# Token numbers written with each batch's placing, and a batch's first load of stage two in two parts

## The chip, the cores and the metric

One core of one Trainium2 chip runs the whole program in one launch. The metric is device time in microseconds (us). The kernel before took 594.89 us (median of three runs, 594.38 to 596.47).

## The reference

`x` (8 batches x 2496 x 256) is filtered along the sequence by FFT, and the 19968 rows that come out go through a mixture of eight experts, one expert for each row:

```python
X = np.fft.rfft(x, axis=1)
y = np.fft.irfft(X * (filt_r + 1j * filt_i)[None], n=2496, axis=1)
logits = y @ w_gate + modality_bias[modality_id]          # (19968, 8)
e = argmax(logits); gate_w = softmax(logits)[e]
out[row] = gate_w * (relu(y[row] @ w1[e]) @ w2[e])        # 256 -> 1024 -> 256
```

## The kernel before

The transform is split as 48 x 52 and runs batch by batch in three stages of matrix products. **Stage 1** (L208) multiplies pieces of `x` and stores the result to DRAM (`b1_d`), one store for every two pieces. A batch has 13 pieces, so its last store holds one piece alone: time steps 24 and 25. **Stage 2** (L532) loads `b1_d` back transposed in three chunks (`load_t2`, L456; partition = 4 x time step + quarter, so the last store's rows are partitions 96 to 103), goes forward (L476), multiplies by the filter and goes back (L488, L489). The result is stored to `b2_d` and loaded back by `load_t4` (L462). **Stage 3** (L551) finishes the transform into `yw`, one of two buffers `yws` (named yo_105 and yo_106 below, used by even and odd batches), and adds up the gate's logits.

Then a batch is **routed**. `counting` (L605) finds each row's expert on VectorE, `placing` (L630) gives every row its place in a bin of its expert, and 20 scatters (L678), issued by GpSimd, write the rows of `yw` into the bins `bins_d`. Beside 256 features a row of `yw` holds its token number, which line 635 writes as one GpSimd instruction over the buffer, and its gate. `tabling` makes a table of full blocks of 256 rows of one expert.

The **experts** take such blocks: SyncE loads one (`xs`, L756), TensorE turns it (L785), multiplies it up (L799, Relu on ScalarE) and down (L812), VectorE scales the result into `osb` (L819, three buffers), and GpSimd scatters it to the output (L821, two to a block) by the token numbers. A block's L819 cannot start until the scatters of the block three before it have landed.

In the main loop (from L1136) the batches overlap. Batch g begins its stage 1 at slot `begin[g]`, 14 slots after the one before; stage 2 follows 16 slots later (`OFF2`), its chunks are loaded two slots ahead (`LEAD`), and routing comes at slot 45. In each slot up to two or three scatters into the bins are traced and 1.5 steps of the experts, four steps to a block.

Up to the main loop the order on TensorE, VectorE and ScalarE is the written one. In the loop a list scheduler sets the order on every engine at build time. It moves an instruction forward as far as its dependencies allow. `paced` (L130) adds one: the instruction waits for the TensorE product traced last. Scatters into the bins and weight loads are paced; line 635 is not. Each engine, and each engine's queue of DMA issues, works in its own order, and an instruction that waits holds what stands behind it.

Of the kernel before, what the change touches and what calls it, by code (L numbers as in the profile page):

```python
# [13 lines left out]
BF16 = mybir.dt.float16  # L14
I32 = mybir.dt.int32
AF = mybir.ActivationFunctionType
ALU = mybir.AluOpType
# [12 lines left out]
def kernel(  # L30
# [12 lines left out]
    nc = tc.nc  # L43

    B, S, D = x.shape
# [12 lines left out]
    NS = N1 // 2  # L58
    NTT = N2 // 2
    KA = 2 * N1  # L60
    KB = 2 * N2
# [15 lines left out]
    DW = D // 2  # L77
# [36 lines left out]
    EV = 2  # L114
# [4 lines left out]
    SCH = 8  # L119
    xp = ctx.enter_context(tc.tile_pool(name="fx", bufs=3))  # L120
    rp = ctx.enter_context(tc.tile_pool(name="fr", bufs=2))
    bp = ctx.enter_context(tc.tile_pool(name="fbig", bufs=4))
# [7 lines left out]
    def paced(ins):  # L130
        tc.add_manual_dep(ins.ins, marks["pe"][-1].name,
                          mybir.DependencyInfo(mybir.DependencyClass.Sync, mybir.DependencyReason.DATA),
                          reason="pace")
# [18 lines left out]
    op = ctx.enter_context(tc.tile_pool(name="opsum", bufs=1, space=bass.MemoryType.PSUM))  # L152
# [35 lines left out]
    st = [dict() for _ in range(B)]  # L188
# [35 lines left out]
    def input_piece(g, k):  # L224

        stage1(g, k)
        if (k + 1) * EV in [t1 for t0, t1 in TCH]:
            load_x()
# [81 lines left out]
    with tc.manual_schedule():  # L310
# [102 lines left out]
        for s0 in range(0, NS, SPB):  # L413
            for src, dst in ((w2m, a1m), (w2x, a2m)):
# [8 lines left out]
                a = 0  # L423
                if s0 == 0:
                    nc.scalar.copy(dst[:, 0, :], tp[:KB, 0:KB])
                    a = 1
# [26 lines left out]
    tp_ = ctx.enter_context(tc.tile_pool(name="table", bufs=1))  # L453


    def load_t2(g, c):  # L456
        src = b1_d[g].rearrange("t (jr s) c -> (t jr) s c", jr=4)
        t2 = bp.tile([KB, SCH, D], BF16, tag="t24", name="t2")
        nc.sync.dma_start(t2, src[:, c * SCH:(c + 1) * SCH, :])
        st[g]["t2", c] = t2  # L460

    def load_t4(g, c):  # L462
        t0, t1 = TCH[c]
        src = b2_d[g].rearrange("s (jr t) c -> (s jr) t c", jr=4)
        t4 = bp.tile([KA, TCM, D], BF16, tag="t24", name="t4")
        nc.sync.dma_start(t4[:, 0:t1 - t0, :], src[:, t0:t1, :])
        st[g]["t4", c] = t4
# [64 lines left out]
    def stage2(g, k):  # L532

        if k < NK:
            ps = forward(g, k)
        if k > 0:
            pz = inverse(g, k - 1)
        if k < NK:
            filtering(g, k, taken(g, k, ps))
        if k > 0:  # L540
            returned(g, k - 1, pz)
# [88 lines left out]
    def placing(g):  # L630

        yw, lg = st[g]["yw"], st[g]["lg"]
        b3 = [P, NY, E]
        mx, ohT, sc, c = st[g]["route"]
        nc.gpsimd.tensor_single_scalar(yw[:, :, DW:DW + 1], tok, g * S, op=ALU.add)
        psO = pp.tile([P, 2, E], F32, tag="ps")
        nc.tensor.matmul(psO[:, 0, :], lhsT=Lexcl, rhs=c, start=True, stop=True)
        nc.tensor.matmul(psO[:, 1, :], lhsT=ones_sq, rhs=c, start=True, stop=True)
        nc.vector.tensor_sub(lg, lg, mx[:, :, None].to_broadcast(b3))
        nc.scalar.activation(lg, lg, AF.Exp)  # L640
        off = sp.tile([P, E], F32, tag="off")
        nc.vector.tensor_add(off, cnt, ecap)
        nc.vector.tensor_add(off, off, psO[:, 0, :])
        nc.vector.tensor_add(cnt, cnt, psO[:, 1, :])
        yield
        nc.vector.tensor_add(sc, sc, off[:, :, None].to_broadcast([P, E, NY]))
        nc.vector.tensor_mul(sc, sc, ohT)
        yield
        pos = sp.tile([P, NY], F32, tag="pos")
        nc.vector.reduce_sum(pos, sc.rearrange("p e t -> p t e"), axis=AX.X)  # L650
        pos_i = sp.tile([P, NY], I32, tag="posi", bufs=2)
        nc.vector.tensor_copy(pos_i, pos)
        st[g]["pos"] = pos_i
        yield
        ssum = sp.tile([P, NY], F32, tag="ssum")
        nc.vector.reduce_sum(ssum, lg, axis=AX.X)
        nc.vector.reciprocal(yw[:, :, DW + 1].bitcast(F32), ssum)
# [6 lines left out]
    def count(g):  # L664

        run(counting(g))

    def place(g):

        run(placing(g))  # L670
# [245 lines left out]
    def pace(left):  # L916

        if to_bins and left:
            g, t = to_bins[0]
            if t < NY:  # L920
                scatter(g, t)
                to_bins[0][1] += 1
                left -= 1
            else:
                if g == B - 1:
                    pad_bins()
                opening.append((g, n))
                to_bins.pop(0)
        return left


    def routed(g):

        place(g)
        to_bins.append([g, 0])

    def tabled(g):

        run(tabling(g, KR[g], g == B - 1))
# [8 lines left out]
    with tc.manual_schedule(engines={ET.PE, ET.Activation, ET.DVE}):  # L948
# [92 lines left out]
        tok = const_pool.tile([P, NY, 1], I32)  # L1041
# [36 lines left out]
        def routes(g):  # L1078

            yield from counting(g)  # L1080
            for _ in range(4):
                yield
            yield from placing(g)
            to_bins.append([g, 0])
            yield
            yield from tabling(g, KR[g], False)
# [20 lines left out]
        for k in range(LONG):  # L1107
# [4 lines left out]
            n += 1  # L1112
        some(-1)
        load_t2(3, 0)
        load_t4(2, 0)
        count(1)
# [11 lines left out]
    LEAD = 2  # L1128
# [7 lines left out]
    while n <= end or to_bins or opening:  # L1136
        if n == 0:
            routed(TURNED - 1)
        if n == 4:
            tabled(TURNED - 1)  # L1140
        for g in range(TURNED + 2, B):
            if 0 <= n - begin[g] < NP:
                input_piece(g, n - begin[g])
        for g in range(TURNED + 1, B):
            k = n - begin[g] - OFF2
            if (k + LEAD) % 4 == 0 and 0 <= k + LEAD < NS // EV:
                load_t2(g, (k + LEAD) // 4)
            if 0 <= k <= NS // EV:
                stage2(g, k)
        for g in range(TURNED, B):  # L1150
            k = n - begin[g] - OFF3
            if (k + LEAD) % 3 == 0 and 0 <= k + LEAD < NPY:
                load_t4(g, (k + LEAD) // 3)
            if 0 <= k <= NPY + 1:
                stage3(g, k)
            if k == NPY + 2:
                count(g)
            if k == NPY + 3:
                routed(g)
                tabled(g)  # L1160
        if n <= end:
            pace(pace(pace(3) if n < 8 else 2) if n % 2 or n < GAP else 1)
            owed += STEPS
        else:
            pace((n - end) % 3)
            owed += FT // FQ
        while owed >= 1:
            owed -= 1
            moe.step()
        n += 1  # L1170
# [43 lines left out]
```

## Time and profile before

| | |
|---|---|
| median of three runs | 594.89 us |
| profiled execution | 592.98 us |
| its span | 591.2 us |
| TensorE busy | 512.1 us (87%) |
| ScalarE, VectorE, GpSimd busy | 379.9, 377.6, 367.4 us |
| GpSimd's 160 scatters into the bins | 162.1 us busy |
| GpSimd's 158 scatters to the output | 160.1 us busy |

The profile's times are from the start of the span; 1.8 us of the execution lie outside of it. PE is TensorE, DVE VectorE, ACT ScalarE, POOL GpSimd and SP SyncE; a "q" behind a name is the engine's sequencer. In a row of the timeline the bracket gives how long the engine stood idle before the instruction and what ended it.

### The profile page before, as it was taken

What the parts mean: (1) busy time and instruction counts of PE and PEld (TensorE: products, weight loads), DVE (VectorE), ACT (ScalarE), POOL (GpSimd) and SP (SyncE); (2) the same over time, 40 slices, a digit from 0 to 9 for tenths busy, and PEclk for the clock granted to TensorE, in tenths of its full rate; (3) what the DMA queues carried; (4) which work ended last, traced back from release to release, by engine and by line L of the source; (5) the groups of instructions that cost most, each with busy time, mean ns of one, the idle gap of its engine ahead of it and who ended that gap; (6) DMA issues with size and microseconds to landing.
All of it is one profiled execution on the core that took longest, in us unless ns stands there. A gap on an engine that the chain in (4) does not pass through costs nothing.

```text
span 591.2 us, 16242 instructions
## 1 busy us (share of the span) xinstructions
PE 512.1 (87%) x5115; PEld 463.2 (78%) x5115; DVE 377.6 (64%) x1209; ACT 379.9 (64%) x693; POOL 367.4 (62%) x409
## 2 busy tenths in 40 slices
PE   3689986739969989999999989966999999999991
PEld 2677875628858888888888978855999999999991
DVE  8557986656766777769679777554555555555541
ACT  4578886827856877777876754433666666666660
POOL 8112336727746776774776776777777777655552
PEclk9969998969998998999998999978999999999997
DMA  8949999887697787898667463224444443333321
GB/s 152 184 68 192 197 212 208 180 204 209 160 239 208 203 198 222 231 211 241 184 176 204 139 165 112 87 86 146 137 127 123 119 125 122 118 109 110 99 73 33
DMA packets 69301, 93.29 MB, mean 158 GB/s; under 512 B 11427, under 2 KB 52841, under 8 KB 69059
## 3 DMA queue, kind: packets, MB, share of 16 engines
q0 software_dynamic: 21504, 50.75, 35.2%
q1 hardware_dynamic: 24409, 29.94, 20.1%
q10 hardware_dynamic: 23302, 11.50, 7.4%
q8 instruction: 48, 0.79, 0.6%
q14 instruction: 38, 0.31, 0.2%
HBM read 64.68 MB, written 46.35 MB: 188 GB/s over the span
## 4 chain that ended last, share of the span: by engine, by line
PE 46%; DMA 20%; issue 11%; POOL 9%; DVE 8%; ACT 3%; SPq 0%; POOLq 0%; DVEq 0%; ACTq 0%
PE hps L799 14%; PE ops L812 13%; POOL out_dram L821 5%; DMA t<-b_d 5%; DMA b_d<-t 3%; DMA bins_d<-yo,pos_i 3%; DMA b_d<-z 3%; PE ps L476 3%; DMA out_dram<-osb,meta 2%; DMA g<-g 2%; PE pz L488 2%; PE lt L584 2%; PE ps L569 2%; PE pz L489 2%; PE pT L785 2%
## 5 line engine op out<-in xcount | busy, mean ns | idle before, releaser
L804 ACT ACTIVATE hT<-hps 128x512 f16<-128x512 f32 x316 | 188.1, 597 | 120.7 <-PE hps L799 118.7
L799 PE MATMUL hps<-xT,w 128*128 128x256 f16 x1264 | 203.6, 282 | 5.7 <-DVE xT L786 5.6
L821 POOL DMA_INDIRECT out_dram<-osb,meta x158 | 160.1, 1014 | 76.4 <-DVE osb L819 36.6
L812 PE MATMUL ops<-w2sb,hT 128*128 x1264 | 198.5, 277 | 2.7 <-issue 2.5
L678 POOL DMA_INDIRECT bins_d<-yo,pos_i x160 | 162.1, 1013 | 56.6 <-issue 19.8
L799 PEld LDWEIGHTS <-w 128*128 128x128 f16 x1264 | 148.1, 146 | 11.0 <-DVE xT L786 6.0
L812 PEld LDWEIGHTS <-hT 128*128 128x128 f16 x1264 | 125.2, 99 | 18.9 <-issue 3.1
L819 DVE TENSOR_SCALAR osb<-ops,meta 128x256 f32<-128x256 f32 x158 | 69.4, 475 | 24.9 <-DMA out_dram<-osb,meta 17.3
L777 DVE COPY w<-w1sb 128x2048 f16 x79 | 56.2, 711 | 42.9 <-PE hps L799 41.1
L786 DVE COPY xT<-pT 128x512 f16<-128x512 f16 x79 | 33.4, 423 | 53.0 <-PE pT L785 52.3
L503 ACT CAST xf<-ps 104x512 f16<-104x512 f32 x96 | 56.9, 592 | 11.5 <-PE ps L476 9.5
L510 DVE TENSOR_TENSOR p<-xf,g 104x512 f16<-104x512 f16 x96 | 40.5, 421 | 36.7 <-ACT xf L503 35.8
L525 ACT CAST z<-pz 104x512 f16<-104x512 f32 x72 | 42.5, 590 | 9.7 <-PE pz L489 8.1
L476 PE MATMUL ps<-t,w2m 104*104 104x256 f16 x192 | 39.9, 292 | 8.7 <-DMA t<-b_d 7.9
L511 DVE TENSOR_TENSOR xf<-xf,g 104x512 f16<-104x512 f16 x96 | 40.5, 421 | 10.0 <-DMA g<-g 6.9
L488 PE MATMUL pz<-p,a1m 104*104 104x256 f16 x144 | 37.5, 284 | 2.7 <-DVE p L510 1.8
L218 ACT CAST t<-ps 96x512 f16<-96x512 f32 x52 | 30.1, 581 | 14.3 <-PE ps L214 12.8
L593 DVE COPY yT<-lt 128x512 f16<-128x512 f16 x80 | 33.5, 419 | 7.1 <-PE lt L589 6.3
L489 PE MATMUL pz<-xf,a2m 104*104 104x256 f16 x144 | 36.6, 280 | 0.0
L785 PE MATMUL pT<-ident,xs 128*128 128x128 f16 x316 | 32.8, 227 | 4.4 <-DMA xs<-bins_d 4.4
L144 POOL DMA_DIRECT2D xt<-in_x_dram x32 | 18.3, 573 | 28.7 <-PE fp L253 14.2
L584 PE MATMUL lt<-ident,yo 128*128 128x128 f16 x320 | 31.4, 221 | 3.7 <-ACT z L525 3.3
(206 smaller groups left out, 725.5 us busy)
## 6 DMA issues: line engine op xcount, KB each, us to landing
xs<-bins_d SPq DMA_DIRECT2D x79, 130.0 KB
xt<-in_x_dram POOLq DMA_DIRECT2D x24, 384.0 KB
t<-b_d SPq DMA_DIRECT2D x18, 384.0 KB
t<-b_d SPq DMA_DIRECT2D x15, 416.0 KB
b_d<-z ACTq DMA_DIRECT2D x30, 208.0 KB
b_d<-t ACTq DMA_DIRECT2D x24, 192.0 KB
w1sb<-in_moe_w_dram POOLq DMA_DIRECT2D x16, 256.0 KB
w2sb<-in_moe_w_dram POOLq DMA_DIRECT2D x8, 512.0 KB
```

Source lines behind the costliest of these rows:

```text
L476: mm = nc.tensor.matmul(ps[:KB, i, :], lhsT=w2m[:, s + i, :], rhs=st[g]["t2", s // SCH][:, s % SCH + i, :], start=True, stop=True)
L488: nc.tensor.matmul(pz[:KB, i, :], lhsT=a1m[:, s + i, :], rhs=p1[:, i, :], start=True, stop=False)
L489: nc.tensor.matmul(pz[:KB, i, :], lhsT=a2m[:, s + i, :], rhs=p2[:, i, :], start=False, stop=True)
L503: nc.scalar.copy(xf, ps[:KB])
L678: ins = nc.gpsimd.indirect_dma_start(out=bins_d[:, :], out_offset=IOA(ap=st[g]["pos"][:rows, t:t + 1], axis=0), in_=st[g]["yw"][:rows, t, ...
L777: cp = nc.vector.tensor_copy(b["w1"].rearrange("p a f -> p (a f)"), w1sb[:, ds(ej, 1)].rearrange("p o a f -> p (o a f)"))
L785: nc.tensor.transpose(pT[:, dc, i, :], xh[:, i, dc * P:(dc + 1) * P], ident)
L799: mm = nc.tensor.matmul(hps[:, k, :], lhsT=b["w1"][:, dc, ft:F:FT], rhs=b["xT"][:, dc].rearrange("p i t -> p (i t)"), start=(dc == 0), sto ...
L804: nc.scalar.activation(b["hT"][:, q * FQ:(q + 1) * FQ, :], hps, AF.Relu)
L812: nc.tensor.matmul(b["ops"][:, i, :], lhsT=b["hT"][:, ft, i * P:(i + 1) * P], rhs=w2sb[:, ds(b["ej"], 1), ft, :], start=(ft == 0 and i == ...
L819: nc.vector.tensor_scalar_mul(osb[:, i, :], b["ops"][:, i, :], gate[:, i, :])
L821: ins = nc.gpsimd.indirect_dma_start(out=out[:, :], out_offset=IOA(ap=b["meta"][:, i, 0:1], axis=0), in_=osb[:, i, :], in_offset=None, bou ...
```

## The change

Three edits. The token numbers' instruction gets `paced`. The load of stage two's first chunk, for the batches that are loaded in the main loop (4 to 7), becomes two: partitions 0 to 95 one slot sooner than the whole was, and partitions 96 to 103, which hold the last store's rows, in the slot of the old load. The other two chunks are loaded as before.

```diff
-    def load_t2(g, c):
+    def load_t2(g, c, part=None):
         src = b1_d[g].rearrange("t (jr s) c -> (t jr) s c", jr=4)
-        t2 = bp.tile([KB, SCH, D], BF16, tag="t24", name="t2")
-        nc.sync.dma_start(t2, src[:, c * SCH:(c + 1) * SCH, :])
-        st[g]["t2", c] = t2
+        if part != 1:
+            st[g]["t2", c] = bp.tile([KB, SCH, D], BF16, tag="t24", name="t2")
+        a, b = {None: (0, KB), 0: (0, KA), 1: (KA, KB)}[part]
+        nc.sync.dma_start(st[g]["t2", c][a:b], src[a:b, c * SCH:(c + 1) * SCH, :])
...
-        nc.gpsimd.tensor_single_scalar(yw[:, :, DW:DW + 1], tok, g * S, op=ALU.add)
+        paced(nc.gpsimd.tensor_single_scalar(yw[:, :, DW:DW + 1], tok, g * S, op=ALU.add))
...
             k = n - begin[g] - OFF2
-            if (k + LEAD) % 4 == 0 and 0 <= k + LEAD < NS // EV:
+            if k + LEAD in (-1, 0):
+                load_t2(g, 0, k + LEAD + 1)
+            if (k + LEAD) % 4 == 0 and 0 < k + LEAD < NS // EV:
                 load_t2(g, (k + LEAD) // 4)
```

TensorE, VectorE and ScalarE keep their orders, instruction for instruction. GpSimd and SyncE change.

GpSimd, where batch 3's scatters end (out of yo_106) and batch 4's begin (out of yo_105), before; `xt` is a load of `x`, TENSOR_SCALAR is the token numbers:

```order
L821 DMA out_dram<-osb,meta 19968x256 x2
L678 DMA bins_d<-yo_106,pos_i 162048x130
L635 TENSOR_SCALAR yo_106<-tok 128x20
L144 DMA xt<-in_x_dram 96x512
L821 DMA out_dram<-osb,meta 19968x256
L678 DMA bins_d<-yo_105,pos_i 162048x130 x2
```

and now:

```order
L824 DMA out_dram<-osb,meta 19968x256 x2
L681 DMA bins_d<-yo_106,pos_i 162048x130
L144 DMA xt<-in_x_dram 96x512
L638 TENSOR_SCALAR yo_105<-tok 128x20
L824 DMA out_dram<-osb,meta 19968x256
L681 DMA bins_d<-yo_105,pos_i 162048x130 x2
```

Before, batch 5's numbers went into the buffer that batch 3's last scatter had just been issued from; now batch 4's go into the other, whose scatters were issued a batch ago.

GpSimd, from batch 4's last scatters to batch 5's first, before:

```order
L678 DMA bins_d<-yo_105,pos_i 162048x130 x3
L821 DMA out_dram<-osb,meta 19968x256 x2
L678 DMA bins_d<-yo_105,pos_i 162048x130 x3
L635 TENSOR_SCALAR yo_105<-tok 128x20
L821 DMA out_dram<-osb,meta 19968x256 x2
L678 DMA bins_d<-yo_106,pos_i 162048x130 x5
```

and now:

```order
L681 DMA bins_d<-yo_105,pos_i 162048x130 x3
L824 DMA out_dram<-osb,meta 19968x256 x2
L681 DMA bins_d<-yo_105,pos_i 162048x130 x3
L638 TENSOR_SCALAR yo_106<-tok 128x20
L824 DMA out_dram<-osb,meta 19968x256 x2
L681 DMA bins_d<-yo_106,pos_i 162048x130 x5
```

The place is the same and the buffer is the other; so it is where batch 6 follows batch 5. Scatters and output scatters keep their order.

SyncE at batch 5's first load of stage two (`t`), before; `xs` are the experts' blocks, L754 and L757 read a block's number:

```order
L756 ISA
L756 DMA xs<-bins_d 128x260
L754 TENSOR_LOAD bj_i
L754 ISA x2
L459 DMA t_4234<-b_d 104x2048
L756 ISA
L756 DMA xs<-bins_d 128x260
```

and now:

```order
L759 ISA
L759 DMA xs<-bins_d 128x260
L463 DMA t_4145<-b_d 96x2048
L757 TENSOR_LOAD bj_i
L757 ISA x2
L463 DMA t_4145<-b_d 8x2048
L759 ISA
L759 DMA xs<-bins_d 128x260
```

The larger part goes ahead of the reading of a block's number, the small one stands where the whole load stood, and no load of `xs` is passed.

## Rows read from the trace of the kernel before

**Rows 1.** The page's chain that ended last: shares of the span by engine

```profile
PE 46%; DMA 20%; issue 11%; POOL 9%; DVE 8%; ACT 3%; SPq 0%; POOLq 0%; DVEq 0%; ACTq 0%
```

**Rows 2.** Waits, whole run: engine, line, waited for: us, times, longest

```profile
POOL yo L635 <- DMA bins_d<-yo,pos_i: 21.1, 5, 6.4
...
DVE osb L819 <- DMA out_dram<-osb,meta: 17.3, 8, 5.5
```

**Rows 3.** Timeline of TensorE: start, us, line, operation, [idle before <- releaser]

```profile
177.28 0.67 PE L476 MATMUL ps<-t,w2m 104*104 104x256 f16 x2 [3.67 <-DMA t<-b_d]
...
222.69 0.38 PE L476 MATMUL ps<-t,w2m 104*104 104x256 f16 x2 [2.68 <-DMA t<-b_d]
...
267.06 0.42 PE L476 MATMUL ps<-t,w2m 104*104 104x256 f16 x2 [0.72 <-DMA t<-b_d]
...
268.41 0.38 PE L476 MATMUL ps<-t,w2m 104*104 104x256 f16 x2
...
388.80 0.60 PE L637 MATMUL psO<-c,Lexcl 128*128 128x8 f32 x2 [5.33 <-DVE c L627]
...
404.39 0.60 PE L799 MATMUL hps<-xT,w 128*128 128x256 f16 x4
...
409.37 1.07 PE L799 MATMUL hps<-xT,w 128*128 128x256 f16 x4 [3.94 <-DVE xT L786]
```

**Rows 4.** Timeline of GpSimd, between one batch's scatters and the next's

```profile
268.61 1.05 POOL L678 DMA_INDIRECT bins_d<-yo,pos_i  x1 [0.30 <-PE ps L214]
276.06 0.32 POOL L635 TENSOR_SCALAR yo<-tok 128x20 int32<-128x20 int32 x1 [6.41 <-DMA bins_d<-yo,pos_i]
...
279.07 0.97 POOL L678 DMA_INDIRECT bins_d<-yo,pos_i  x1 [0.30 <-PE ps L476]
...
316.63 0.91 POOL L678 DMA_INDIRECT bins_d<-yo,pos_i  x1 [0.30 <-issue]
...
323.65 0.97 POOL L678 DMA_INDIRECT bins_d<-yo,pos_i  x1 [0.30 <-PE pT L785]
...
359.51 1.33 POOL L678 DMA_INDIRECT bins_d<-yo,pos_i  x1 [0.30 <-issue]
...
367.13 0.98 POOL L678 DMA_INDIRECT bins_d<-yo,pos_i  x1 [0.30 <-PE lt L589]
...
404.07 1.00 POOL L821 DMA_INDIRECT out_dram<-osb,meta  x1 [0.30 <-issue]
```

**Rows 5.** Timeline of VectorE: the experts' results and a batch's places

```profile
271.66 0.47 DVE L819 TENSOR_SCALAR osb<-ops,meta 128x256 f32<-128x256 f32 x1
...
315.53 0.17 DVE L652 CAST pos_i<-pos 128x20 int32<-128x20 f32 x1
...
355.79 0.17 DVE L652 CAST pos_i<-pos 128x20 int32<-128x20 f32 x1
...
384.67 0.88 DVE L819 TENSOR_SCALAR osb<-ops,meta 128x256 f32<-128x256 f32 x2 [4.41 <-DMA out_dram<-osb,meta]
...
407.95 0.88 DVE L819 TENSOR_SCALAR osb<-ops,meta 128x256 f32<-128x256 f32 x2 [5.51 <-DMA out_dram<-osb,meta]
```

**Rows 6.** Issue of batch 4's last store but one, on ScalarE's queue

```profile
161.74 0.31 ACTq L221 DMA_DIRECT2D b_d<-t  x1
```

**Rows 7.** The chain that ended last, in order of time: start, us, what

```profile
165.97 6.64 DMA b_d<-t
172.68 4.57 DMA t<-b_d
...
211.34 5.45 DMA b_d<-t
...
384.54 2.29 DMA bins_d<-yo,pos_i
```

**Rows 8.** Stretches: us, busy us (count) by PE, PEld, DVE, ACT, POOL; PEclk, DMA share, GB/s

```profile
160.00:182.00 22.00, 17.17 (x143) 14.41 (x141) 14.17 (x57) 12.95 (x25) 9.26 (x11) 0.87 0.97 252
...
410.00:500.00 90.00, 90.00 (x841) 83.62 (x839) 48.27 (x120) 55.52 (x93) 69.12 (x69) 0.97 0.42 127
```

## The prediction

> **What bounds the kernel now.** I read the chain that ended last first. TensorE holds 46% of it, DMA 20% and GpSimd 9% [rows 1]: products are the floor, and what can be won is where TensorE waits. From 410 to 500 us it is busy for 90.00 of 90 us [rows 8], and it stays so to its last products. So every us that TensorE loses before 410 is a us at the end, and only those count.
>
> TensorE's timeline shows the losses. At 177.28, 222.69 and 267.06 it waits 3.67, 2.68 and 0.72 us for the first load of stage two of batches 4, 5 and 6 [rows 3]. At 388.80 and 409.37 it waits 5.33 and 3.94 us for VectorE [rows 3]; a third such wait of about 1.2 us lies between them. VectorE's own timeline says why: at 384.67 and 407.95 it stood 4.41 and 5.51 us in front of L819 because an `osb` buffer was not yet scattered to the output [rows 5]. Over the run this wait comes to 17.3 us in 8 times [rows 2]. So GpSimd is late there, though its share of the chain is small.
>
> Its timeline tells where it fell behind. Between one batch's last scatter and the next one's first it stands still in front of the token numbers, 6.41 us at batch 4 and 21.1 us in 5 times [rows 2, 4], until the scatters just issued have let go of the buffer. Within a batch's scatters it never idles longer than the 0.30 us between two instructions, so from 279 us on it has no room to catch up.
>
> **The token numbers.** Eight instructions of about 0.3 us stay; what goes is the wait for a buffer's own scatters. The other buffer, which is now written, was scattered a batch ago. I give the first two of the five waits nothing: the scatters behind them start where their batch's places are made, and GpSimd has caught up when they end. I count the last three, from one scatter's end to the next batch's first scatter [rows 4]. With d for what TensorE is ahead by the stage-two loads:
>
> - Batch 4: 269.66 to 279.07. Now an `x` load (0.9), the numbers (0.6 with the gap) and one output scatter (1.29) stand between. That scatter needs the first half of the `osb` made at 271.66 to 272.13 [rows 5], so batch 4 starts at 273.8 - d. Gain 5.3 + d.
> - Batch 5: 317.54 to 323.65, 6.1 us. Numbers 0.6 and two output scatters 2.6 remain, so it would start at 315.4 - d, but the places are there at 315.70 - d [rows 5]. Gain then 7.9 + d.
> - Batch 6: 360.84 to 367.13, 6.3 us, against 3.2. The places come at 355.96 - d [rows 5], GpSimd at 356.1 - d. Gain then 11.0 + d.
>
> After it GpSimd runs the same scatters at the same pace, so the output scatter at 404.07 [rows 4] starts 11.0 + d sooner. The wait added is for a product. For batch 4 it is the product at 268.41 [rows 3], and GpSimd is there at about 269.7 - d or later; for batches 5 to 7 it comes later still against its product. Behind the waiting instruction stand an `x` load and output scatters, and VectorE waits for these; a late mark would cost its lateness. Bounds: 0, and 2 us where GpSimd is ahead; I take 0, since it is the one that is late.
>
> TensorE must be able to use it. Without late outputs it would get back 4.4 of the 5.33 us (I leave 0.9 for VectorE's counting, which it still has to await), 1.2 and 3.9. It runs at the lower of its two clock levels after each of the two long waits: four products take 1.07 us at 409.37 against 0.60 at 404.39 [rows 3], some 2 us lost each. That is about 14 us, more than 11.0, so GpSimd sets what is won. One wait remains in part: the `osb` wait at 407.95 would end at 407.95 - 11.0 - d, while VectorE gets there, at 402.44 before, about 4.4 + 1.2 + 2.5 + d sooner. That leaves some 2.6 us of the 5.51.
>
> **The load in two parts.** Now the last store takes 6.64 us to land, the load behind it 4.57 us, and TensorE starts [rows 7]. Of the load only 32 KB remain behind the store. No row shows so small a load. Bounds: 2.29 us, the landing of a 66 KB scatter [rows 7], and 4.57, the whole load. I take 2.4, near the scatter. The 384 KB ahead go off when the store before has landed: that one was issued at 161.74 [rows 6], so with 6.64 us they start at 168.4 and land by 173 to 175.
>
> What it costs: they now share the DMA with the last store, where the DMA share is 0.97 and 252 GB/s move [rows 8]. If the store lands behind all of them it is late by 384 KB / 252 GB/s = 1.6 us; if not, by nothing. I take 0.5. A rule bears on this. The Trainium skill ("DMA: Bandwidth & Descriptors", Queues, rings and completion order) says that each DMA engine goes round-robin between the queues that have work, a packet at a time, so loads and stores of two issuing engines take turns. By that rule the 96 KB store meets at most about its own size of the load, an estimated 0.4 us, and the sum below would be 16.3; with the store behind the whole load it would be 14.3. No row here shows the turns.
>
> Batch 4: 172.6 + 0.5 + 2.4 = 175.5 instead of 177.28, gain 1.8 (0.6 to 2.3). Batch 5: the store lands at 216.8 [rows 7], then 219.7; TensorE is free at 220.0, gain 2.6 (1.8 to 2.68). Batch 6: the wait of 0.72 goes. Batch 7 did not wait. d = 5.0, from 3.1 to 5.7. SyncE issues four loads more at about 0.4 us each and passes none by; reading a block's number now stands between the parts, and the wait for the store covers it.
>
> **Sum.** 11.0 + 5.0 = 16.0 us off 592.98, that is 577.0 for an execution like the profiled one. The median of the runs shown lies 1.9 us above it: 579.
>
> **Rivals.**
> A. The store is slowed by the load, or the small load takes as long as the whole: d = 0 and only GpSimd's part stays. For it: the DMA share of 0.97. Against it: 32 KB are half of the scatter that landed in 2.29 us. Gain 11.0, 584.
> B. GpSimd's lateness costs nothing that can be won, because the waits at 388.80 and 409.37 come back as others (counting, places, loads of blocks). For it: GpSimd is on only 9% of the chain. Against it: VectorE's waits name the output scatters. Only d stays: 590.
> C. Slower: scatters and output scatters that run 8 to 11 us sooner meet the stores and loads of stages one to three, whose pairs are on the chain (6.64 and 4.57 us at batch 4). If each of the four pairs that end a wait of TensorE grows by half, 5 us, that is 20 against 11, about 604. It decides from 2.8 us for each pair. Against it: the same bytes move, only sooner, and the share falls from 0.97 at 160 to 0.42 after 410 [rows 8].
> D. The change doesn't do what it says: GpSimd comes to the numbers before their product, and waits as long for it as it did for the scatters. Then 594 to 595. Against it: 268.41 lies ahead of GpSimd's arrival.
>
> **How the numbers follow.** Forecast 0.62, A 0.14, B 0.12, C 0.07, D 0.05. The forecast's own range is 573 to 584: TensorE's limit (14 + 5 + up to 2 of low clock after 177.28) below, d = 3.1 and some lateness above. To hold eight in ten it takes in A and part of B: 573 to 590. A measurement of this kernel can tell about 0.3%, 1.8 us, from no change. Faster by more: 0.88 (forecast, A, B); the same: 0.05 (D); slower: 0.07 (C).
>
> **What would show it.** GpSimd: no idle time over 1 us in front of the token numbers after 200 us, and 0.3 us for each of them. VectorE: waits for output scatters down from 17.3 to under 6 us. TensorE: the wait at batch 5's first stage-two products gone, batch 4's near 2 us, the one ahead of batch 7's counting near 1. Loads of 32 KB landing within 2.3 to 3 us of the last store. It would be wrong if TensorE still stood 3 us or more twice between 370 and 400, if the numbers waited for TensorE, or if the last store's landing grew by over 1.5 us.

## The result

The changed kernel takes 586.34 us (median of four runs, 584.62 to 587.38) where the kernel before takes 595.47 (four runs, 594.38 to 596.47): 0.984 of its time, 95% interval 0.981 to 0.988. It is faster, inside the stated range, and by 9.1 us where 16.0 were forecast. The profiled execution took 585.33 us with a span of 583.2, that is 7.7 and 8.0 us less than before.

On the chips of the experiments the kernel before varied more (585.89 to 601.13), so two medians that lie 2 us apart aren't told apart there by one series; the ratios leave the longest executions out as disturbed, in the first series 11 of the kernel before's 23, and so can lie nearer 1 than the medians do.

GpSimd first. In the changed kernel's waits (engine, line, waited for: us, times, longest) the 21.1 us in front of the token numbers [rows 2] are gone; two waits for TensorE's products, in the opening and at batch 2, remain. VectorE's waits for the output scatters stand almost as they were:

```profile
DVE osb L822 <- DMA out_dram<-osb,meta: 16.5, 10, 5.5
...
POOL yo L638 <- PE ps L214: 4.8, 1, 4.8
...
POOL yo L638 <- PE fp L214: 1.5, 1, 1.5
```

GpSimd's timeline in the changed kernel shows the starts of batches 4, 5 and 6 (L681 after L638), which answer to 279.07, 323.65 and 367.13 [rows 4]:

```profile
270.41 0.28 POOL L638 TENSOR_SCALAR yo<-tok 128x20 int32<-128x20 int32 x1
273.26 1.07 POOL L824 DMA_INDIRECT out_dram<-osb,meta  x1 [2.56 <-DVE ni L708]
274.63 1.07 POOL L681 DMA_INDIRECT bins_d<-yo,pos_i  x1 [0.30 <-issue]
...
313.00 0.28 POOL L638 TENSOR_SCALAR yo<-tok 128x20 int32<-128x20 int32 x1
...
317.00 0.97 POOL L681 DMA_INDIRECT bins_d<-yo,pos_i  x1 [1.09 <-issue]
...
354.90 0.28 POOL L638 TENSOR_SCALAR yo<-tok 128x20 int32<-128x20 int32 x1
...
357.97 1.08 POOL L681 DMA_INDIRECT bins_d<-yo,pos_i  x1 [0.30 <-PE ps L575]
```

The numbers take 0.28 us and wait for nothing. The three batches start 4.4, 6.7 and 9.2 us sooner.

TensorE's timeline in the changed kernel, at the places of [rows 3] and at a new one:

```profile
176.74 0.39 PE L479 MATMUL ps<-t,w2m 104*104 104x256 f16 x2 [2.29 <-DMA t<-b_d]
...
220.28 0.38 PE L479 MATMUL ps<-t,w2m 104*104 104x256 f16 x2 [1.83 <-DMA t<-b_d]
...
229.60 0.39 PE L572 MATMUL ps<-t,wbm 96*128 96x256 f16 x1 [3.41 <-DMA t<-b_d]
...
382.56 0.39 PE L640 MATMUL psO<-c,Lexcl 128*128 128x8 f32 x2 [0.85 <-DVE c L630]
...
399.88 1.07 PE L802 MATMUL hps<-xT,w 128*128 128x256 f16 x4 [3.74 <-DVE xT L789]
```

The 5.33 us at 388.80 have shrunk to 0.85 and the 0.72 us at batch 6 are gone. The waits at batches 4 and 5 are smaller. At 229.60 TensorE stands 3.41 us for the first load of stage three (`load_t4`), where the kernel before did not wait for the same product:

```profile
229.96 0.28 PE L569 MATMUL ps<-t,wbm 96*128 96x256 f16 x1
```

TensorE's order is the same in all the kernels here, so every product can be compared with itself. The table gives how much later (+) or sooner (-) than in the kernel before the same product starts, in us, for the products that started there at the times of the first row (388.8 is the one behind the wait of 5.33 us). It is worked out from the profiled executions, so each row holds an accident as well: at 150 us, before the waits in question, the rows lie between -1.9 and +1.4.

| | 150.3 | 228.1 | 245.0 | 268.1 | 350.8 | 388.8 | 415.1 | last |
|---|---|---|---|---|---|---|---|---|
| changed kernel | -1.1 | -3.9 | +0.4 | +0.2 | -0.4 | -6.2 | -10.6 | -9.7 |
| the same, again | -1.4 | -5.8 | +0.2 | -0.1 | -0.1 | -6.0 | -9.2 | -8.5 |
| token numbers only | -0.2 | +0.5 | +0.8 | +0.8 | +0.8 | -4.8 | -9.2 | -8.0 |
| load in two parts only | +0.4 | -2.5 | +2.2 | +0.7 | +1.0 | +0.6 | -2.0 | -0.9 |
| two parts, stage three's load ahead | +1.4 | +1.7 | +1.3 | +1.3 | +1.7 | -0.5 | -1.8 | -0.8 |
| changed, stage three's load ahead | -0.5 | -3.0 | -1.9 | -2.6 | -3.8 | -8.2 | -13.3 | -10.5 |
| the same, again | +1.4 | -1.6 | +0.5 | 0.0 | +1.2 | -4.5 | -11.2 | -6.8 |
| that, load in three parts | -0.4 | -4.9 | -2.8 | -3.3 | -2.5 | -7.6 | -12.3 | -12.0 |
| that in two parts, four osb buffers | +1.2 | -1.6 | -1.2 | -2.0 | -3.1 | -7.9 | -18.8 | -16.1 |
| before, four osb buffers | -1.5 | -1.2 | +3.0 | +2.5 | +2.3 | -1.4 | -8.0 | -3.6 |
| all edits | -1.9 | -3.8 | -3.5 | -3.9 | -4.6 | -9.1 | -20.3 | -16.6 |

The first two rows tell the story. What the load in two parts won by 228 us was gone at 245. All that remains was won between 350 and 415, and that is GpSimd's part.

Why the load at 229.60 was late can be read in the changed kernel. Its chain that ended last (start, us, what), which answers to 211.34 [rows 7], with SyncE waiting at the end of it:

```profile
209.86 6.49 DMA b_d<-t
216.37 0.02 SPq L463
216.41 3.82 DMA t<-b_d
...
222.64 0.18 SPq L759
...
223.72 5.83 DMA t<-b_d
```

and SyncE's timeline of the same stretch (L463 stage two's load, L759 `xs`, L469 stage three's load):

```profile
209.49 7.25 SPq L463 DMA_DIRECT2D t<-b_d  x2
222.46 0.36 SPq L759 DMA_DIRECT2D xs<-bins_d  x1
223.72 0.31 SPq L469 DMA_DIRECT2D t<-b_d  x1
224.07 0.50 SPq L463 DMA_DIRECT2D t<-b_d  x1
224.92 0.30 SPq L469 DMA_DIRECT2D t<-b_d  x1
```

An `xs` load stands ahead of stage three's load and gets away only at 222.46. Three loads of about 400 KB then go off within 1.2 us, and the first takes 5.83 us. In the kernel before stage three's load was issued 1.9 us later:

```profile
225.64 0.34 SPq L466 DMA_DIRECT2D t<-b_d  x1
```

There it landed after 3.81 us, at 229.45, and TensorE reached its first product at 229.96 without waiting: the load came just in time. So TensorE, 3.9 us ahead, met a load that was sent 1.9 us sooner but took 2.0 us longer (5.84 in the second profile of the changed kernel), and that landed at the same time as before, 229.55. Why it took longer isn't shown. The wait costs more than itself. Stretches (us, busy us and count by PE, PEld, DVE, ACT, POOL; PEclk, DMA share, GB/s), first one of the kernel before, then the changed kernel's:

```profile
224.00:226.00 2.00, 2.00 (x14) 1.83 (x13) 2.00 (x11) 1.14 (x3) 1.45 (x2) 0.52 0.25 64
```

```profile
224.00:226.00 2.00, 2.00 (x20) 1.91 (x18) 2.00 (x13) 1.94 (x5) 1.07 (x2) 1.00 1.08 240
...
229.60:231.00 1.40, 1.40 (x7) 1.02 (x8) 0.33 (x1) 0.00 (x0) 0.99 (x1) 0.50 0.97 275
231.00:234.00 3.00, 3.00 (x22) 2.68 (x21) 1.49 (x7) 1.26 (x3) 0.96 (x1) 0.72 0.92 249
```

Behind it the granted clock is 0.50 of full speed (the lower level) and then 0.72: at that speed 4.4 us hold the work of 2.9, some 1.5 us more. The kernel before paid this sooner, at 0.52 behind its wait of 2.68 us at 222.69, where the changed kernel, after a wait of 1.83, kept 1.00. So part of the lead at 228 was clock that was not lost, and it was lost after all at the next wait.

### The profile page after: what moved, and what is told of

Read it like the earlier page. It is cut to its first block, busy times and chain, and to the rows that moved or that the text cites. A ratio compares the mean times of both kernels' runs of the same rounds, so it can differ in the third digit from the quotient of the medians.

```text
span 583.2 us, 16257 instructions
## 1 busy us (share of the span) xinstructions
PE 503.1 (86%) x5115; PEld 456.4 (78%) x5115; DVE 376.4 (65%) x1209; ACT 378.8 (65%) x693; POOL 369.0 (63%) x409
## 4 chain that ended last, share of the span: by engine, by line
PE 48%; DMA 18%; issue 11%; POOL 8%; DVE 8%; ACT 3%; SPq 1%; DVEq 0%; POOLq 0%; ACTq 0%
PE hps L802 14%; PE ops L815 14%; POOL out_dram L824 5%; DMA t<-b_d 4%; DMA b_d<-t 4%; DMA bins_d<-yo,pos_i 3%; PE lt L587 3%; PE ps L479 2%; PE ps L572 2%; DMA g<-g 2%; PE pz L491 2%; PE pz L492 2%; PE ps L575 2%; DMA out_dram<-osb,meta 2%; PE pT L788 2%
## 5 line engine op out<-in xcount | busy, mean ns | idle before, releaser
L802 PE MATMUL hps<-xT,w 128*128 128x256 f16 x1264 | 199.8, 277 | 7.4 <-DVE xT L789 5.6
L681 POOL DMA_INDIRECT bins_d<-yo,pos_i x160 | 164.3, 1027 | 66.0 <-issue 22.2
L815 PE MATMUL ops<-w2sb,hT 128*128 x1264 | 196.0, 274 | 3.6 <-issue 3.4
L802 PEld LDWEIGHTS <-w 128*128 128x128 f16 x1264 | 146.4, 146 | 12.7 <-DVE xT L789 6.2
L822 DVE TENSOR_SCALAR osb<-ops,meta 128x256 f32<-128x256 f32 x158 | 69.3, 474 | 23.8 <-DMA out_dram<-osb,meta 16.5
L514 DVE TENSOR_TENSOR xf<-xf,g 104x512 f16<-104x512 f16 x96 | 40.4, 421 | 10.6 <-DMA g<-g 7.5
L572 PE MATMUL ps<-t,wbm 96*128 96x256 f16 x120 | 29.7, 278 | 5.4 <-DMA t<-b_d 5.3
```

The lines of the kernel that those rows point to most:

```text
L681: ins = nc.gpsimd.indirect_dma_start(out=bins_d[:, :], out_offset=IOA(ap=st[g]["pos"][:rows, t:t + 1], axis=0), in_=st[g]["yw"][:rows, t, ...
L802: mm = nc.tensor.matmul(hps[:, k, :], lhsT=b["w1"][:, dc, ft:F:FT], rhs=b["xT"][:, dc].rearrange("p i t -> p (i t)"), start=(dc == 0), sto ...
L815: nc.tensor.matmul(b["ops"][:, i, :], lhsT=b["hT"][:, ft, i * P:(i + 1) * P], rhs=w2sb[:, ds(b["ej"], 1), ft, :], start=(ft == 0 and i == ...
L822: nc.vector.tensor_scalar_mul(osb[:, i, :], b["ops"][:, i, :], gate[:, i, :])
```

## Experiments

**The token numbers alone.** The load of the first chunk is whole again.

```diff
-            if k + LEAD in (-1, 0):
-                load_t2(g, 0, k + LEAD + 1)
-            if (k + LEAD) % 4 == 0 and 0 < k + LEAD < NS // EV:
+            if (k + LEAD) % 4 == 0 and 0 <= k + LEAD < NS // EV:
```

> Only the token numbers' edit; the first load of stage two is whole again, as before. Theory: TensorE's order is one chain, the 3.6 us that the split won by 228 us were lost again at the next load (a wait of 3.41 us at 229.60), so GpSimd's part is the whole gain of 9: 586 +- 1.5, with the 177, 222 and 267 us waits back (3.7, 2.7, 0.7) and none at the first load of stage three. Rival 1, the forecast's sum (11.0 for the numbers alone): 584. Rival 2, the split did harm that it did not pay for: 583 or less. Rival 3, the numbers need TensorE's lead to pay: 589 or more.

Measured: 586.64 us against 594.57 (ratio 0.993, 0.989 to 0.997), the profiled span 583.2, the same as the changed kernel's. Batch 6's scatters start at 357.99, as there. TensorE's timeline:

```profile
177.56 0.67 PE L479 MATMUL ps<-t,w2m 104*104 104x256 f16 x2 [4.03 <-DMA t<-b_d]
...
223.17 0.38 PE L479 MATMUL ps<-t,w2m 104*104 104x256 f16 x2 [2.83 <-DMA t<-b_d]
...
383.97 0.39 PE L640 MATMUL psO<-c,Lexcl 128*128 128x8 f32 x2 [0.84 <-DVE c L630]
...
400.46 1.08 PE L802 MATMUL hps<-xT,w 128*128 128x256 f16 x4 [4.33 <-DVE xT L789]
```

The waits of stage two are back, nothing is lost near 230, and the 5.33 us at 388.80 are gone all the same. The time is that of the theory, and rivals 1 and 2 are further from it; rival 3 falls by the median and by the trace, in which the wait goes without any lead of TensorE. How large a share of the gain this edit is stays open. By the medians it is 7.9 us, where the changed kernel's is 9.1 and, in its second series below, 9.9; by the ratio it is 0.7% (some 4 us) against 1.6% in both series, and the intervals hardly meet. TensorE's last product came 8.0 us sooner, against 9.7 and 8.5. So it is most of the gain by the medians and the traces, and that it is the whole isn't shown.

**The load in two parts alone.**

```diff
-        paced(nc.gpsimd.tensor_single_scalar(yw[:, :, DW:DW + 1], tok, g * S, op=ALU.add))
+        nc.gpsimd.tensor_single_scalar(yw[:, :, DW:DW + 1], tok, g * S, op=ALU.add)
```

> Only the load in two parts; the token numbers are as before. Theory: won by 228 us, lost at 229.60, so within 1.5 us of before: 594 to 596, with a new wait of about 3 us at the first load of stage three near 230 us and GpSimd's five waits of 21 us still there. Rival 1, the forecast's sum (d = 5.0): 590. Rival 2, the split does harm by sharing the DMA with the last store: 597 or more.

Measured: 592.63 us against 594.57, ratio 1.001 (0.997 to 1.005). TensorE and the chain:

```profile
178.02 0.64 PE L479 MATMUL ps<-t,w2m 104*104 104x256 f16 x2 [4.79 <-DMA t<-b_d]
...
230.84 0.28 PE L572 MATMUL ps<-t,wbm 96*128 96x256 f16 x1 [3.24 <-DMA t<-b_d]
```

```profile
165.63 10.24 DMA b_d<-t
175.89 2.00 DMA t<-b_d
```

The new wait for stage three's load is there (3.24 us), and alone the edit is worth nothing that can be measured (the median lies 1.4 us under the 594 to 596 of the theory, the ratio at no change). Here the larger part went off with batch 4's last store: the store took 10.24 us to land, against 6.64 before [rows 7]. The small part's 2.00 us did not pay for that, and the wait at batch 4 grew to 4.79.

**Stage three's load ahead of `xs`.** At batches 3, 4 and 7 the `xs` load that stood ahead of it goes behind up to three loads; the other engines keep their orders.

```diff
+        if c == 0 and g > TURNED:
+            marks["t4"] += [ld.ins] * 2
...
-        ld = nc.sync.dma_start(xs, binv[ds(bj, 1)].rearrange("o p i d -> p (o i) d"))
+        with behind("t4" if len(marks["t4"]) == 1 else "none", 1): ld = nc.sync.dma_start(xs, binv[ds(bj, 1)].rearrange("o p i d -> p (o i) d"))
...
-        marks["ld"].append(ld.ins)
+        marks["ld"].append(ld.ins); del marks["t4"][-1:]
```

> The changed kernel, with the first load of stage three put ahead of the one xs load that SyncE issued before it (at batches 3, 4 and 7; xs goes behind up to three loads). Theory: at 222.46 SyncE stood for a buffer of xs and the load of stage three stood behind it until 223.72; sooner and without that xs beside it, it lands 2.5 to 4 us sooner, the wait of 3.41 us goes to under 1, and 583 comes out (2 to 4 less than the changed kernel). Rival 1: that load waits for the last store of stage two or for DMA rate, not for its place on SyncE: the wait stays over 2.5 us, 586. Rival 2: the xs that is now late makes TensorE wait for its block, 588 or more.

Measured: 581.88 us against 594.57 (ratio 0.984, 0.976 to 0.993). SyncE and TensorE:

```profile
222.09 0.30 SPq L469 DMA_DIRECT2D t<-b_d  x1
222.48 0.39 SPq L463 DMA_DIRECT2D t<-b_d  x1
222.92 0.34 SPq L469 DMA_DIRECT2D t<-b_d  x1
223.77 1.96 SPq L759 DMA_DIRECT2D xs<-bins_d  x2
```

```profile
176.55 0.64 PE L479 MATMUL ps<-t,w2m 104*104 104x256 f16 x2 [4.18 <-DMA t<-b_d]
...
221.17 0.38 PE L479 MATMUL ps<-t,w2m 104*104 104x256 f16 x2 [1.80 <-DMA t<-b_d]
...
234.04 0.27 PE L572 MATMUL ps<-t,wbm 96*128 96x256 f16 x1 [0.96 <-ACT t L218]
```

The load goes off 1.6 us sooner, lands at 226.97 just before its product at 227.02, and no product waits for it. In the table the lead of 3.0 us at 228 now stays until 350. Rivals 1 and 2 fall in the trace. To set the times side by side the changed kernel and this one ran together:

> The changed kernel itself, on the chip of the next three kernels, so that they can be set beside it. 586, with waits of 1.5 to 2.5 us at the first products of stage two of batches 4 and 5 and of about 3.4 us at the first load of stage three near 230 us.

> The kernel with the first load of stage three ahead of the xs load, once more, beside the changed kernel. Theory: 3 to 5 us under the changed kernel (581 to 583), without a wait near 228 us at the first load of stage three. Rival, the difference between the two before was chance: within 1.5 us of it.

Measured: 584.95 and 583.52 us against 594.84 (0.985, 0.979 to 0.990, and 0.980, 0.975 to 0.985). The waits came as expected in the changed kernel (2.44, 1.61 and 3.60 us), and in the other there was none over 0.2 us for stage three's load near 230. But 1.4 us between the medians is less than the 3 to 5 expected, and doesn't settle the size. In this execution two other things took the lead (1.6 us at 228) back: at 236.72 TensorE stood 2.40 us for ScalarE, which itself waited for a store of 10.54 us that met the three loads; and from 410 on it stood 1.82 and 1.97 us for VectorE behind late outputs.

**Three parts.** On top of that, 256 KB two slots sooner, 128 KB one slot sooner, 32 KB last.

```diff
-        a, b = {None: (0, KB), 0: (0, KA), 1: (KA, KB)}[part]
+        a, b = {None: (0, KB), 0: (0, 64), 1: (64, KA), 2: (KA, KB)}[part]
...
-            if k + LEAD in (-1, 0):
-                load_t2(g, 0, k + LEAD + 1)
+            if k + LEAD in (-2, -1, 0):
+                load_t2(g, 0, k + LEAD + 2)
```

> The kernel above, with the first load of stage two in three parts: partitions 0 to 63 (256 KB) two slots sooner, 64 to 95 (128 KB) one slot sooner, 96 to 103 (32 KB) last, so that 128 KB instead of 384 KB go beside the last store. Theory: the store's small packets wait for those of the load, so the last store lands in 5 to 7 us where it took 9.79 at batch 4 and 6.54 at batch 5 when the 384 KB went off with it; the wait for the first load of stage two shrinks from 4.2 and 1.8 us to under 1.5 each, and 2 to 4 us come off (578 to 580). Rival 1: the store is slow for other reasons (x loads, scatters, xs): its landing and the waits stay, within 1 us of the kernel above. Rival 2: a load more in front of two xs loads makes a block late: 1 us or more slower.

Measured: 582.06 us against 594.84 (ratio 0.978, 0.972 to 0.984). No product of stage two waits for its load any more; the longest waits of TensorE from 170 to 250 us are for others:

```profile
173.71 0.55 PE L640 MATMUL psO<-c,Lexcl 128*128 128x8 f32 x2 [2.21 <-DVE c L630]
...
233.54 0.27 PE L572 MATMUL ps<-t,wbm 96*128 96x256 f16 x1 [2.59 <-ACT t L218]
```

The last store landed after 7.10 us at batch 4 and 2.51 at batch 5, where the repeat above had 9.21 and 3.92 and the theory asked for 5 to 7. That agrees with the theory, but it is one execution: in the kernel with all edits, which has the three parts too, the last stores took 5.83 and 5.46 us and waits of 0.59 and 1.64 us for the load came back. Behind these waits VectorE's counting and ScalarE come next, and the time falls by 1.5 us where 2 to 4 were expected, which isn't settled against chance.

**Four `osb` buffers.** With stage three's load ahead (two parts), and one `xs` buffer less to make room.

```diff
-        xs = ep.tile([P, NI, RW], I32, tag="xs", bufs=5)
+        xs = ep.tile([P, NI, RW], I32, tag="xs", bufs=4)
...
-            osb = ep.tile([P, NI, D], F32, tag="osb", bufs=3)
+            osb = ep.tile([P, NI, D], F32, tag="osb", bufs=4)
```

> The kernel with the first load of stage three ahead, with four osb buffers and, to make room, four xs buffers instead of five. It asks whether GpSimd's lateness still costs after the change, by VectorE's 16.5 us of waits for osb between 389 and 420 us. Theory: yes; with a block more of slack these waits fall to under 8 us, TensorE's 3.7 us near 400 go, and 2 to 5 us come off (577 to 580). Rival 1: the waits were off TensorE's path, or come later at GpSimd's pace: no change, 581 to 583. Rival 2: one xs buffer less makes blocks late: 584 or more.

Measured: 580.95 us against 594.84 (ratio 0.976, 0.970 to 0.982). TensorE's timeline and the wait:

```profile
398.05 0.66 PE L802 MATMUL hps<-xT,w 128*128 128x256 f16 x4 [0.78 <-DVE xT L789]
...
406.98 0.66 PE L802 MATMUL hps<-xT,w 128*128 128x256 f16 x4 [0.94 <-DVE xT L789]
```

```profile
DVE osb L822 <- DMA out_dram<-osb,meta: 12.4, 10, 3.1
```

VectorE still waits 12.4 us (under 8 were expected), but at most 3.1 us at a time instead of 5.5, and TensorE no longer stands 3.7 us. So in the trace GpSimd's lateness still cost TensorE time after the change. The median lies 2.6 us under the repeat of the kernel that it builds on, which alone isn't settled against chance, and with one `xs` buffer less SyncE's loads come in another order too.

**Two parts with stage three's load ahead, token numbers as before.**

> The load in two parts and the first load of stage three ahead of xs, with the token numbers as before. It asks whether the split keeps what it wins once the load behind it is not late. Theory: 2 to 4 us less than before (590.5 to 592.5), no wait at the first load of stage three near 230 us, and GpSimd's late outputs back at 385 to 410 us. Rival 1, the forecast's d = 5.0 was right and only that load hid it: 589 to 590. Rival 2, what is won there is lost anyway between 230 and 390 us: 594 to 595.

Measured: 592.68 us against 594.90, ratio 0.999 (0.996 to 1.002); it lies between theory and rival 2, and by the ratio on the rival's side. In its profiled execution there is no wait near 230, but batch 4's store took 9.65 us, batch 5's 7.88, and nothing was ahead at 228. What GpSimd does to TensorE is that of [rows 3] again:

```profile
388.28 0.59 PE L640 MATMUL psO<-c,Lexcl 128*128 128x8 f32 x2 [5.32 <-DVE c L630]
...
408.70 0.66 PE L802 MATMUL hps<-xT,w 128*128 128x256 f16 x4 [3.83 <-DVE xT L789]
```

**Four `osb` buffers in the kernel before.** The two lines of the experiment above, in the kernel before.

> The kernel before, with four osb buffers and four xs buffers; token numbers and loads as before. Theory: GpSimd's lateness reaches TensorE only through osb, so a block more of slack gives back a part of what the token numbers' edit did: TensorE's waits of 5.33 and 3.94 us at 388.80 and 409.37 shrink by half or more together, and 3 to 6 us come off (589 to 592), with GpSimd's 21 us in front of the token numbers unchanged. Rival 1: GpSimd is a full batch behind and the fourth buffer only moves the wait: within 1.5 us of before. Rival 2, four xs buffers are too few: 597 or more.

Measured: 591.04 us against 594.90 (ratio 0.995, 0.992 to 0.999). GpSimd's wait in front of the token numbers stays (19.0 us in 5 times), and TensorE's waits shrink:

```profile
387.40 0.39 PE L640 MATMUL psO<-c,Lexcl 128*128 128x8 f32 x2 [0.96 <-DVE c L630]
...
402.45 0.71 PE L802 MATMUL hps<-xT,w 128*128 128x256 f16 x4 [2.69 <-DVE xT L789]
410.15 0.66 PE L802 MATMUL hps<-xT,w 128*128 128x256 f16 x4 [2.10 <-DVE xT L789]
```

The time is in the theory's range. A block more of slack shrinks the wait at 388.80 to 0.96 us as the token numbers' edit does, though GpSimd waits as before: it is through `osb` that its lateness reaches TensorE.

**All edits.** The changed kernel with three parts, stage three's load ahead, four `osb` and four `xs` buffers.

> The changed kernel with the three further edits together: the first load of stage two in three parts, the first load of stage three ahead of xs, four osb and four xs buffers. Theory: the edits win at different places (175 to 230 us and 385 to 410 us), so they add up: 577 to 580, 5 to 8 us under the changed kernel. Rival: with TensorE ahead GpSimd is the bound again, and it comes out as with the four osb buffers alone, 581.

Measured: 576.35 us (572.72 to 578.48) against 594.90, ratio 0.972 (0.966 to 0.978): faster than both kernels, and its interval lies below those of the changed kernel (0.981 to 0.988, and 0.979 to 0.990 in its second series). In the table the lead of the loads (3.8 us at 228) is kept to 350 and the outputs' comes on top, so the edits win at different places. A wait for another load of stage three is new, 2.04 us at 349.52 (with the three parts alone it was 1.37). How far they add up isn't settled: the kernel with two parts and four `osb` buffers has an interval of 0.970 to 0.982, which meets this one's, and its last product came 16.1 us sooner, where it is 16.6 here. So the rival's 581 is missed by the median, but that the three parts add to the four buffers isn't shown.

## Why the prediction was right, and where its size failed

**The range.** The forecast was 579 and its own range 573 to 584. The 586.34 measured lies outside of that, and inside the stated range only because this takes in rival A and part of B.

**The token numbers, 11.0 us: right in kind, about 2 too large.** GpSimd's lateness between two batches was the cost, it went where it was expected, and alone it is most of the change. Batch 6 starts 9.2 us sooner. The steps were 4.4 where 5.3 + d stood, 2.2 more at batch 5 (2.6), 2.5 more at batch 6 (3.1). At batch 4 the output scatter that goes first stood 2.56 us until 273.26: TensorE was 0.2 us late there instead of 5.0 ahead, so there was no lead to start from. The wait added cost nothing, as taken: in the changed kernel the numbers wait for no product after 200 us.

**The load in two parts, d = 5.0: this step failed.** By the end of it d was about zero. Two things went wrong.

*It was worth half or less.* From the last store's issue to the first products' data batch 4 took 11.3, 12.0 and 13.2 us with the whole load (kernel before, token numbers only, four `osb` buffers in the kernel before), 12.2 on average. In seven executions with two parts it took 9.4 to 13.9, on average 11.5. For batch 5 the averages are 11.2 (three) and 9.9 (seven, 8.8 to 11.6). That is 0.6 and 1.3 us where 1.8 and 2.6 were forecast, and the 0.6 is well within the spread. The two terms were mis-sized in opposite ways. The small load was sized well at batch 4 (2.0 to 2.7 us, 2.4 taken) and not at batch 5 (3.6 to 5.2). The store, for which 0.5 us was taken and 1.6 was the bound, landed after 7.15 us on average at batch 4 with the whole load (6.64 to 7.55) and 9.30 with two parts (7.36 to 11.18): 2.15 us more, past the bound, and past the 1.5 us that the prediction named as a sign of being wrong. At batch 5 it was 4.4 and 5.6 us. In all seven executions the larger part and the store landed within 0.8 us of each other at batch 4.

The sentence on the round of the queues misread the rule. The Trainium skill ("DMA: Bandwidth & Descriptors", Queues, rings and completion order) speaks of turns by packets, and the prediction made of it turns by bytes. The DMA view of the changed kernel from 208 to 232 us (queue: packets, MB, share) shows how unlike the packets are; by the bytes issued there q1 carries SyncE's loads and q10 ScalarE's stores:

```profile
q1 hardware_dynamic: 890, 2.03, 32.0%
q10 hardware_dynamic: 2202, 1.08, 15.9%
```

On the stores' queue a packet is 490 bytes on average, on the loads' 2.3 KB. If turns go by these packets, a store gives way to several times its own size. The longer landings agree with that, but no run here changed the packets alone, so that the turns are the cause isn't shown.

*What it won was lost at the next load.* The prediction asked what is late next behind GpSimd, and did not ask it here. The row to read was the load of stage three, which in the kernel before landed 0.5 us before its product, and which SyncE issues behind an `xs` load that waits for its buffer. The 3.41 us at 229.60 and the lower clock behind it (some 1.5 us) gave back all that the split had won. With that load ahead, five executions came to 228 us with a lead: three kept it (the first series, four `osb` buffers, all edits), three parts kept half, and the repeat lost it to ScalarE behind a slow store.

**The sum.** 16.0 was 11.0 + 5.0; it came to 9.7 for TensorE's last product, and 8.0 for the span, since 14.0 us lay behind that product where there had been 12.3. This end took 12.3 us in five of the executions profiled and 13.7 to 14.1 in seven, whatever the edit (the changed kernel has 14.0 and 12.3), so this 1.7 is an accident of the one profile; the medians' 9.1 stands nearer to TensorE's 9.7.

**The rivals.** A, the load gives nothing, is what happened in total (584 by its sum, 586.34 measured), but its reason, the slowed store, is only a part of it. B falls with the experiment on the token numbers. C falls: the kernel is not slower, and from the last store's issue to the first products' data batches 4 and 5 took 9.4 and 10.4 us, where it had been 11.3 each time. D falls with GpSimd's timeline.

**What was to show it.** Right: no idle time before the token numbers, 0.28 us each; the wait before batch 7's counting, 0.85 us; batch 4's wait near 2 (2.29). Wrong: VectorE's waits for the outputs are 16.5 us, not under 6. This goes against the prediction's own sentence that GpSimd sets what is won: as long as it does, VectorE comes sooner by as much and waits as long. Wrong too: batch 5's wait is 1.83 us, not gone, and its small load landed in 3.82 us instead of 2.3 to 3.

## What to carry to other kernels

A gain on the engine that never idles is kept only up to the next thing that came just in time; so after each wait that is removed, look for the loads behind it that landed within the gain, and at what stands ahead of them on their queue. When the lateness of an engine is passed on through a ring of buffers, a buffer more and an engine less late are two ways to the same wait; here either took the 5.33 us at 388.80 down to under 1. Before a load is sent off early beside the store that it is split from, allow for a slower store: here it landed after 9.30 us instead of 7.15.

## What was not expected of the hardware

- A store of 96 KB at batch 4 took 2.15 us longer to land on average (9.30 against 7.15 us, seven and three executions) when a load of 384 KB went off beside it.
- A load of 32 KB took 2.0 to 2.7 us at one place and 3.6 to 5.2 at another, where the whole 416 KB took 4.6 to 5.5 and 5.7 to 8.5.
- A store of 192 KB that met three loads of about 400 KB each near 225 us took 9.3 to 11.4 us to land in five kernels, and ScalarE stood behind it. Beside the same loads it took 7.3 and 8.6 us in two others and 4.1 in the kernel before, so the loads alone don't set it.
